# Two more groups of token pairs with seven products each, and the exits and squares shared between two engines

## The chip, the core and the metric

The kernel runs on one core of a Trainium2 chip. The metric is the device time of one execution in microseconds (us); lower is better. The engines are called as the profile calls them: PE is the matrix engine, DVE the vector engine, ACT the scalar engine, POOL the GpSimd engine, SP the engine that issues most DMAs. Each works through its own list of instructions in order and waits on semaphores of the others.

## What is computed

```python
scores = q @ k.transpose(0, 1, 3, 2) / 8              # q, k, v: (8, 12, 448, 64)
x = (np.maximum(scores, 0) ** 2 / 448 @ v)            # then heads side by side: (8, 448, 768)
u = x + np.real(fft(fft(x, axis=1), axis=2))
un = (u - mean(u)) / sqrt(var(u) + 1e-6)              # over the last axis
out = u + np.maximum(un @ w_ch1, 0) @ w_ch2           # 768 -> 3072 -> 768
```

An attention with squared relu, a Fourier mix over tokens and channels, and a feed-forward network (FFN) over 3584 tokens.

## The kernel before

**Order.** The order of work is written by a planner inside the kernel. Each piece of work is a generator that yields `need(engine, duration, dependencies, buffers)`; `Streams.run` (L80) picks the piece that can start first and issues its instructions. So the order on each engine is fixed when the program is built, from the planner's own durations; on the chip only semaphores move it.

**Attention** (`attention`, L526). Per batch 24 score blocks of 112 keys x 2 heads x 448 queries, in visits of up to three: six score matmuls (L591), then ACT takes the relu out of PSUM (L615) and DVE squares it in place (L621). Four squares feed one value product of 8 matmuls (L574) into a `psF` bank, of which there are two, shared with the FFN. DVE takes that product out in two halves of 224 columns (L475 and L479, in `fold`, L466) and folds it (L498, L500). SP turns the halves with DMA transposes (L521). There are 9 buffers for squares up to batch 3, and 6 from batch 4.

**Mix** (`mix` L1023, `mix_rows` L860). Channel transform (L1039), then for two chunks of rows the token transform (L868), a sum and a difference (L877, L879), the sum with x into `u` (L888, L890 on POOL and DVE), statistics (L903), and the normalized `un` (L920 on POOL; for batch 1 L923 on ACT, and turned by PE into `unT` at L837 and L842). `u` and `un` go to DRAM (L942 by SP, L945 by POOL); from batch 2 on `un` comes back turned by DMA (`turns`, L968, L986). `u` and `un` have two sets of buffers up to batch 3 and one from batch 4.

**FFN** (`ffn`, L1194). Tokens go in 12 groups: 384, 512, 384 and then nine of 256. Per group the first product (L1243, 24 rows of 128 hidden channels) goes through a relu (L1218 on ACT; in group 0 half of them L1216 on DVE) into `hT`. The second product of the first three groups is plain (L1274): 48 matmuls of 384 columns per block of 128 tokens. A group of 256 is one *pair* of blocks (class `Pair`, L1330): with the hidden channels halved (even and odd) and the output halved, the 2x2x2 block product is done with seven block products instead of eight, 84 matmuls instead of 96. That needs sums of hidden blocks, made by DVE for every pair (`early` L1312 to L1316, `late` L1324), and sums of weight blocks, made once by DVE (`weight_sums`, L1127), in buffers that other things have left. L1229 (DVE) adds each product to `u` in the output buffer `o`.

Of the kernel before, what the change touches and what calls it, by code (L numbers as in the profile page):

```python
# [62 lines left out]
class Streams:  # L63
# [9 lines left out]
    def dma(self, start, nbytes, rate=350e3, queue="hw"):  # L73
        slow = queue == "hw" and self.dma_free["sw"] > start + 2.0
        self.dma_free[queue] = max(self.dma_free[queue], start + 1.0) + nbytes / rate * (2.0 if slow else 1.0)
        if slow:
            self.dma_free["sw"] += nbytes / rate
        return self.dma_free[queue] + (3.0 if slow else 2.2 if queue == "sw" else 1.2)

# [63 lines left out]
def kernel(  # L143
# [27 lines left out]
    GT = [0, 384, 896] + list(range(1280, B * S + 1, 256))  # L171
# [129 lines left out]
    def home(i):  # L301

        return (i - NG) % 2 if i < 4 * NG else 1
# [96 lines left out]
    def turning():  # L400

        for b in range(B):
            for g in range(NG):
# [5 lines left out]
                for x in range(2):  # L409
                    e = yield need("DVE", 0.42, [ready[b * NG + g][x]], [BQR] if x == 0 else [])  # L410
                    o = work.tile([R, 4, HG, Dh], BF16, name="qkr", tag=f"qkr{x}", bufs=QR)
                    nc.vector.tensor_copy(o, loads[b * NG + g][x])  # L412
                    if b * NG + g != 4 * NG - 1:
                        BQ[x][home(b * NG + g)].free.append(e)
                    else:
                        qk_left.t = e + LATENCY["DVE"]
                    qk.append(o.rearrange("p c h d -> p (c h d)"))
# [48 lines left out]
    def fold(b, m, F, av, av_end):  # L466
# [4 lines left out]
        def leave():  # L471

            t = yield need("DVE", 2 * dve(HS) + 2 * dve2(NS) if one else dve(HS), [av_end],
                           [BX[m]] + ([BA[m]] if m < 3 else []))
            nc.vector.tensor_scalar(x[:, 0:HS].rearrange("q (p j) -> q p j", j=4), at[:, 0:R // 2],  # L475
                                    1.0 / (64.0 * S), None, op0=ALU.mult)
            t = yield from next_step(b, "DVE", dve(HS), t)
            xb, ab = x[:, XH + 1:XH + NS].rearrange("q (p j) -> q p j", j=4), at[:, R - 1:R // 2 - 1:-1, ::-1]
            nc.vector.tensor_scalar(xb, ab, 1.0 / (64.0 * S), None, op0=ALU.mult)  # L479
            t2 = t - 2 * dve2(NS) if one else t  # L480
            BF.give(av, t2)
            if b > 0:
                sch.add(turn_x(b, m, t2 + LATENCY["DVE"]), (1, 1))
            else:
                x_ready[b][m].t = t + LATENCY["DVE"]
            gone.t = t
            return t

        if one:
            e1 = yield from leave()  # L490
        else:
            sch.add(leave(), (0, 0))
            yield need("SP", 0.0, [gone])
            e1 = gone.t
        f = work.tile([128, 2, NS], BF16, name="fold", bufs=1,
                      tag=f"diff{m - 3}" if b == 0 and m >= 3 else f"fold{min(m, 3)}")
        e1 = yield from next_step(b, "DVE", dve2(NS), e1)
# [17 lines left out]

    def turn_x(b, m, t):

        e = yield need("SP", 0.5, [t], [BXN] if m == 0 else [])
        if m == 0:
            xns[b] = work.tile([128, 4, D], BF16, name="xn", tag="xn", bufs=1)  # L520
# [5 lines left out]
    def attention(b):  # L526


        F, sqs, fresh = [], {}, []
        if b == 4:  # L530
# [6 lines left out]
        while pa < NB:  # L537
            few = b == 0 or progress[0] == 0.0
# [7 lines left out]
            values = values or not n  # L546
            fresh.append(p + n)
            deps, bufs, dur = [], [], 0.0
            if values:
                deps += [sqs[i][1] for i in range(pa, pa + 4)]  # L550
# [3 lines left out]
                deps.append(ready[b * NG + ma // 2][2])  # L554
# [5 lines left out]
            lead = b + (p if n else pa) / NB - LEAD  # L560
# [5 lines left out]
            for part in ("scores", "values") if few else ("values", "scores"):  # L566
                if part == "values" and values:
                    av = BF.take()
                    vn, h0 = loads[b * NG + ma // 2][2], 2 * ma % HG
                    for c in range(4):  # L570
                        sq, _, at = sqs.pop(pa + c)
# [6 lines left out]
                    if ma % 2 == 1:  # L578
                        BQ[2].free.append(e)
                    pa += 4  # L580
# [22 lines left out]
            if scs:  # L603
                sch.add(squares(scs, sqs), (0.2, 0.2))
            if av_end is not None:
                yield from fold(b, ma, F, av, av_end)

    def squares(scs, sqs):
        for i, sc, t in scs:
# [7 lines left out]
            sch.add(square(r, e + LATENCY["ACT"], sqs[i][1]), (0.2, 0.2))  # L617

    def square(r, t, done):
        e = yield need("DVE", dve2(2 * S), [t])  # L620
        nc.vector.tensor_tensor(r, r, r, op=ALU.mult)  # L621
        done.t = e + LATENCY["DVE"]

    def attentions():
        for b in range(1, B):
            yield from attention(b)
# [4 lines left out]
    def side(b, ch):  # L631

        return ch if b < 4 else 1
# [226 lines left out]
    def mix_rows(b, ch, pcs):  # L860
# [3 lines left out]
        e = yield need("PE", 4 * mm(KN), [pcs[0][1], pcs[1][1]], [BS])  # L864
# [7 lines left out]
        e = yield need("ACT", act(KN), [e + LATENCY["PE"]], [BTS])  # L872
# [35 lines left out]
        e = yield need("DVE", 0.3, [e3 + LATENCY["ACT"]], [BUN[ch if b < 4 else 0]])  # L908
# [5 lines left out]
        for i, u in enumerate(us):  # L914
# [3 lines left out]
            un = work.tile([128, D], BF16, name="un", tag=f"un{2 * (ch if b < 4 else 0) + i}", bufs=1)  # L918
# [31 lines left out]
    def u_store(b, ch, us, ut, freed):  # L950
        yield from store_rows(ch, utop[b], ubot[b], us, 4, ut, u_stored[b])
        yield need("SP", 0.0, freed)
        for i in range(2):
            t = max(u_stored[b][2 * ch + i].t, freed[i].t)
            BU[i][side(b, ch)].free.append(t)
            if b == 3 and ch == 0:
                u_left[i].t = t

    def n_store(b, ch, t):
        yield from store_rows(ch, ntop[b], nbot[b], uns[b][2 * ch:2 * ch + 2], 2,  # L960
                              [t, t], n_stored[b])
        if b > 0:
            if b == 3 and ch == 1:
                un_left.t = n_stored[b][3].t
            else:
                BUN[ch if b < 3 else 0].free.append(n_stored[b][2 * ch + 1].t)

    def turns():  # L968

        pair_homes = None  # L970
        for k in range(2, NGR):
            t, g = GT[k], None
            while t < GT[k + 1]:
# [5 lines left out]
                e = yield need("SP", 1.5, deps, [BUNT] if g is None else [])  # L979
                if g is None and k == 2:  # L980
                    g = work.tile([128, MC, 512], BF16, name="unT", tag="unT0", bufs=1)
# [10 lines left out]
    def second_turned():  # L992
# [4 lines left out]
        BUN[1].free.append(e)  # L997
        group_ready[1].t = e
# [87 lines left out]
    PLAIN = (0, 1, 2)  # L1086
# [11 lines left out]
    unt_left, w2_free = Cell(), Cell()  # L1098
# [5 lines left out]
    def weight_sums():  # L1104
# [38 lines left out]
        yield from several(1, b12, b12, b11, ALU.subtract, [w2_free])  # L1143
        t4 = upper(JC * 256, KP, DH)
        yield from several(4, [(t4, i) for i in range(KP)], b21, t2, ALU.subtract, [w2_free])

    def uses():

        at, odd = [], 0
        for g in range(NGR):  # L1150
            n = (GT[g + 1] - GT[g]) // 128
            for c in range(0, n, 1 if g in PLAIN else 2):
                if g in PLAIN:
                    at += [(g, c, hf, (0, 1, 2, 3, 5)[(len(at) + hf) % 5]) for hf in range(2)]
                else:
                    at += [(g, c, 0, 0), (g, c + 1, 0, 1 + odd), (g, c + 1, 1, 3 + odd), (g, c, 1, 5)]
                    odd = 1 - odd
        return at
# [35 lines left out]
    def ffn(b):  # L1194
# [4 lines left out]
        flat = hid[0].rearrange("p j n -> p (j n)")  # L1199
        h = hid[0] if b in PLAIN else flat[:, 0:JC * 256].rearrange("p (j n) -> p j n", n=256)  # L1200
        ht = [Cell() for _ in range(JC)]
        work_us = JC * MC * mm(N) + NC * (2 * JC - (0 if b in PLAIN else KP // 2)) * mm(DH)
# [7 lines left out]
        def relu(ph, e, j):  # L1210

            en = "DVE" if b == 0 and j % 2 else "ACT"
            e = yield need(en, (dve if en == "DVE" else act)(JN * N), [e + LATENCY["PE"]], BH[j:j + JN])
            hs, ps = h[:, j:j + JN, 0:N], ph[:, 0:JN * N].rearrange("p (j n) -> p j n", j=JN)
            if en == "DVE":
                nc.vector.tensor_scalar(hs, ps, 0.0, None, op0=ALU.max)  # L1216
            else:
                nc.scalar.activation(hs, ps, AF.Relu)  # L1218
# [3 lines left out]

        left = {(c, hf): 1 if b in PLAIN or (c % 2, hf) == (0, 1) else 2 for c in range(NC) for hf in range(2)}

# [12 lines left out]
        for j in range(0, JC, JN):  # L1237
# [9 lines left out]
            if j == JC // 2:  # L1247
                ffn_begun[b].t = e
                if b not in PLAIN:
                    pairs = [Pair(b, c, h, ht, add, advance) for c in range(0, NC, 2)]  # L1250
                    for p in pairs:
                        sch.add(p.early(), (0, 0.3))
                        sch.add(p.late(), (0, 0.3))
        if b == 2:
# [4 lines left out]
        if b not in PLAIN:  # L1259
            for p in pairs:  # L1260
                sch.add(p.chain_a(), (4, 0))
                sch.add(p.chain_b(), (3.9, 0))
                yield need("SP", 0.0, p.done)
            for x in BH:
                x.free.append(max(d.t for d in p.done))
            return
        for c in range(NC):
            for hf in range(2):
                for jq in range(4):
# [3 lines left out]
                    for j in range(6 * jq, 6 * jq + 6):  # L1273
                        nc.tensor.matmul(pc[:, 0:DH], lhsT=h[:, j, c * 128:(c + 1) * 128], rhs=w2(j, hf),  # L1274
# [5 lines left out]
        if b == 2:  # L1280
            w2_free.t = e + LATENCY["PE"]

    class Pair:
# [14 lines left out]
        def early(self):  # L1298
# [110 lines left out]
    LEAD = 2.6  # L1409
# [50 lines left out]
```

## Time and profile before

| | us |
|---|---|
| runs shown: median, lowest to highest | 593.81, 592.65 to 594.01 |
| the profiled execution's own time | 595.38 |
| its span (first to last instruction) | 593.6 |
| PE busy in the span | 581.6 (98%) |
| DVE, ACT, POOL busy | 400.7, 292.4, 158.8 |
| matmuls of the second product: L1274, L1330 | 480, 756 |

Times below are from the span's start. "Busy" of PE is the time in which a matmul is under way. "Granted clock" is the share of full speed that PE was given.

### The profile page before, as it was taken

How to read it: one execution, taken by the hardware profiler on the slowest of the kernel's cores; microseconds unless marked ns; L12 is line 12 of the kernel's file. 1: busy time of each engine (PE TensorE's matmuls, PEld its weight loads, DVE VectorE, ACT ScalarE, POOL GpSimd, SP SyncE). 2: the span in 40 equal slices, each digit the busy share in tenths (PEclk: the TensorE clock that was granted, in tenths of full speed). 3: DMA queues.
4: the chain of work that ended last, by engine and by line, in shares of the span. 5: the costliest groups of instructions: out<-in, count | busy, mean ns of one | idle time of the engine just before them, and what ended most of it. 6: DMA issues, size and time to landing. Idle time of an engine off the chain costs nothing.

```text
span 593.6 us, 11558 instructions
## 1 busy us (share of the span) xinstructions
PE 581.6 (98%) x4522; PEld 370.8 (62%) x4522; DVE 400.7 (68%) x925; ACT 292.4 (49%) x433; POOL 158.8 (27%) x200
## 2 busy tenths in 40 slices
PE   8999999989999999999999999999999999999997
PEld 6566556534455465556757667566675686868684
DVE  6976775954678768877986877767898576232323
ACT  5966672467645557544617536275276340404040
POOL 8433112410236117312641134301260025000000
PEclk9998999989999999999999999999999999999999
DMA  9999999845958998888559967749264134221111
GB/s 126 207 210 228 210 213 143 190 81 90 170 117 177 208 141 216 136 162 136 141 141 166 140 127 207 126 100 175 102 181 87 53 120 151 75 84 47 66 43 53
DMA packets 133493, 82.29 MB, mean 139 GB/s; under 512 B 77504, under 2 KB 128608, under 8 KB 133440
## 3 DMA queue, kind: packets, MB, share of 16 engines
q0 software_dynamic: 40320, 34.07, 36.6%
q1 hardware_dynamic: 93120, 47.50, 35.2%
q8 instruction: 35, 0.57, 0.4%
q14 instruction: 18, 0.15, 0.1%
HBM read 62.91 MB, written 26.69 MB: 151 GB/s over the span
## 4 chain that ended last, share of the span: by engine, by line
PE 88%; DVE 5%; ACT 3%; POOL 2%; issue 2%; DMA 0%; DVEq 0%; POOLq 0%
PE psF L1243 35%; PE psF L1330 20%; PE psF L1274 13%; PE psF L574 7%; PE psS L591 6%; PE psS L1039 2%; ACT sq L615 2%; DVE sq L621 1%; PE psS L868 1%; PE psS L667 1%; POOL un L920 1%; PE psS L1014 1%; PE psF L448 0%; DVE o L1229 0%; DMA out_dram<-o 0%
## 5 line engine op out<-in xcount | busy, mean ns | idle before, releaser
L1243 PE MATMUL psF<-unT,w 128*128 128x256 bf16 (+2 forms) x1728 | 231.7, 292 | 1.8 <-ACT unT L842 1.7
L615 ACT ACTIVATE sq<-psS 112x896 bf16<-112x896 f32 x192 | 164.5, 916 | 93.3 <-PE psS L591 89.9
L1243 PEld LDWEIGHTS <-w 128*128 128x128 bf16 x1728 | 166.2, 98 | 64.5 <-issue 18.5
L1218 ACT ACTIVATE hT<-psF 128x512 bf16<-128x512 f32 (+1 forms) x168 | 96.7, 576 | 119.8 <-PE psF L1243 117.5
L621 DVE TENSOR_TENSOR sq<-sq 112x896 bf16<-112x896 bf16 x192 | 118.9, 633 | 36.1 <-ACT sq L615 35.6
L1330 PEld LDWEIGHTS <-hT 128*128 128x128 bf16 x648 | 62.9, 98 | 43.8 <-issue 2.3
L1274 PE MATMUL psF<-w,hT 128*128 128x384 bf16 x480 | 82.1, 326 | 0.0
L1229 DVE TENSOR_TENSOR o<-psF,o 128x384 f32<-128x384 f32 x83 | 45.8, 552 | 45.7 <-PE psF L1330 40.7
L1330 PE MATMUL psF<-w,hT 128*128 128x384 bf16 x378 | 66.4, 326 | 1.4 <-DVE xT L479 0.8
L1274 PEld LDWEIGHTS <-hT 128*128 128x128 bf16 x480 | 45.5, 98 | 34.5 <-issue 6.1
L591 PE MATMUL psS<-qkT 64*128 64x448 bf16 (+1 forms) x384 | 50.9, 359 | 1.6 <-ACT qkT L453 0.4
L319 POOL DMA_DIRECT2D vn<-in_v_dram x24 | 17.3, 720 | 115.6 <-PE psS L591 82.6
L574 PE MATMUL psF<-sq,vn 112*64 112x448 bf16 x384 | 45.5, 358 | 0.5 <-ACT hT L1218 0.5
L920 POOL TENSOR_SCALAR un<-u,rstd,nmr 128x768 bf16<-128x768 f32 (+1 forms) x24 | 29.6, 1241 | 42.4 <-DVE nmr L912 42.3
L475 DVE TENSOR_SCALAR xT<-psF 128x224 bf16<-128x224 f32 x48 | 18.6, 388 | 31.1 <-PE psF L574 30.6
L888 POOL TENSOR_TENSOR u<-tp,xn 128x385 f32<-128x385 f32 (+1 forms) x14 | 13.7, 978 | 84.0 <-DVE tp L877 76.5
L591 PEld LDWEIGHTS <-qkT 64*128 64x128 bf16 (+1 forms) x384 | 16.1, 102 | 28.2 <-issue 21.2
L574 PEld LDWEIGHTS <-vn 112*64 112x64 bf16 x384 | 17.8, 109 | 21.0 <-issue 12.1
L319 POOL DMA_DIRECT2D qn<-in_q_dram x21 | 15.1, 719 | 54.8 <-DVE qkr L412 46.1
L1330 PE MATMUL psF<-wsum,hT 128*128 128x384 bf16 x162 | 28.6, 326 | 0.0
L903 DVE BATCH_NORM_STATS2 stats<-u 128x6 f32<-128x384 f32 (+1 forms) x56 | 28.6, 539 | 0.0
L945 POOL DMA_INDIRECT ubot<-u,back x16 | 18.2, 1137 | 24.1 <-DVE sq L621 19.6
(141 smaller groups left out, 526.7 us busy)
## 6 DMA issues: line engine op xcount, KB each, us to landing
out_dram<-o SPq DMA_DIRECT2D x56, 192.0 KB
vn<-in_v_dram POOLq DMA_DIRECT2D x24, 224.0 KB, 5.4
qn<-in_q_dram POOLq DMA_DIRECT2D x21, 224.0 KB, 5.3
kn<-in_k_dram POOLq DMA_DIRECT2D x21, 224.0 KB, 8.1
w<-in_moe_w_ch_dram POOLq DMA_DIRECT2D x12, 384.0 KB, 13.2
w<-in_moe_w_ch_dram POOLq DMA_DIRECT2D x4, 1152.0 KB, 27.4
utop<-u SPq DMA_DIRECT2D x8, 384.0 KB
o<-utop SPq DMA_DIRECT2D x16, 192.0 KB
```

Of the source, the lines that this page charges most:

```text
L319: nc.gpsimd.dma_start(out=t, in_=src[b, hs].rearrange("h (p j) d -> p h (j d)", j=4))
L574: nc.tensor.matmul(av[h * Dh:(h + 1) * Dh, 0:S], lhsT=vn[:, c, h0 + h, :], rhs=sq[:, h, :], start=(c == 0), stop=(c == 3))
L591: nc.tensor.matmul(sc[:wide, h, 0:S].rearrange("k (c q) -> k c q", c=4), lhsT=flat[ps, k0:k0 + wide], rhs=qT[ps, m % 2], start=True, stop= ...
L615: nc.scalar.activation(r, sc[:R, :, 0:S], AF.Relu)
L621: nc.vector.tensor_tensor(r, r, r, op=ALU.mult)
L903: nc.vector.bn_stats(stats[:n, hf, :], u[:n, hf * (D // 2):(hf + 1) * (D // 2)])
L920: nc.gpsimd.tensor_scalar(un[:n], u[:n], rstd[:n, i:i + 1], nmr[:n, i:i + 1], op0=ALU.mult, op1=ALU.add)
L1218: nc.scalar.activation(hs, ps, AF.Relu)
L1229: nc.vector.tensor_tensor(o, pc[:, 0:DH], o, op=ALU.add)
L1243: nc.tensor.matmul(ph[:, i * N:(i + 1) * N], lhsT=w1_sb[m][hf][:, (jj + i) * 128:(jj + i + 1) * 128], rhs=unT[:, m, 0:N], start=(m == 0), ...
L1274: nc.tensor.matmul(pc[:, 0:DH], lhsT=h[:, j, c * 128:(c + 1) * 128], rhs=w2(j, hf), start=(j == 0), stop=(j == JC - 1))
L1330: nc.tensor.matmul(pc[:, 0:DH], lhsT=lhs[i], rhs=rhs[i], start=(start and i == 0), stop=(i == KP - 1), skip_group_check=True)
```

## The change

The last group now has 384 tokens and the third 256: groups are 384, 512, nine of 256, 384. Pairs begin with group 1: its first two blocks are a pair, its other two are done *whole*. In the last group two blocks are a pair and one is whole. Only group 0 stays plain. A whole block has 48 matmuls and an extra DVE add: as the weight sum of the upper and lower output half replaces one of the weight blocks in place, one product is shared by both halves. Everything that was switched at batch 4 (room for squares, single buffers of `u`, `un`, q and k) is switched at batch 2 (`ONE`) or batch 3 (`ONEQ`), since weight sums lie in those buffers earlier. From batch 1 on the second half of each exit of x is taken by ACT, and a square goes to ACT where the planner finds that sooner: 9 of 192. The last value product of a batch may wait for the first visit of the next.

```diff
-    GT = [0, 384, 896] + list(range(1280, B * S + 1, 256))
+    GT = [0, 384] + list(range(896, B * S - 383, 256)) + [B * S]
+    ONE, ONEQ = 2, 3
...
-        return (i - NG) % 2 if i < 4 * NG else 1
+        return (i - NG) % 2 if i < ONEQ * NG else 1
...
+            if b == 0:
...
+            else:
+                t = yield need("DVE", dve(HS), [av_end], [BX[m]] + ([BA[m]] if m < 3 else []))
+                nc.vector.tensor_scalar(xa[0], xa[1], 1.0 / (64.0 * S), None, op0=ALU.mult)
+                t2 = yield need("ACT", act(HS), [av_end])
+                nc.scalar.activation(xb[0], xb[1], AF.Copy, scale=1.0 / (64.0 * S))
+                t = max(t, t2 + LATENCY["ACT"] - LATENCY["DVE"])
...
-        room = NSQ if b < 4 else NSQ - 3
+        room = NSQ if b < ONE else NSQ - 3
...
+    def sooner(t, other, d, usual, du):
+
+        wait = {en: max(t, sch.engine[en]) + sch.queued(en) for en in (other, usual)}
+        return wait[other] + d + SPARE < wait[usual] + du
+
+    def square(b, r, t, done):
+        if b >= ELASTIC[0] and sooner(t, "ACT", act(2 * S), "DVE", dve2(2 * S)):
+            e = yield need("ACT", act(2 * S), [t])
+            nc.scalar.activation(r, r, AF.Square)
+        else:
+            e = yield need("DVE", dve2(2 * S), [t])
+            nc.vector.tensor_tensor(r, r, r, op=ALU.mult)
...
-        return ch if b < 4 else 1
+        return ch if b < ONE else 1
...
-        e = yield need("PE", 4 * mm(KN), [pcs[0][1], pcs[1][1]], [BS])
+        e = yield need("PE", 4 * mm(KN), [pcs[0][1], pcs[1][1]], [BS, BTS])
...
-    PLAIN = (0, 1, 2)
+    WHOLES = [[0, 1, 2], [2, 3]] + [[]] * (NGR - 3) + [[2]]
+    PAIRS = [[], [0]] + [[0]] * (NGR - 2)
...
+        yield need("DVE", 0.0, [upper_free])
         t4 = upper(JC * 256, KP, DH)
...
+            if b == 1:
+                moves = [(halves[:, :, j], ph.rearrange("p (x n) -> p x n", x=2))]
+            elif b == NGR - 1:
+                moves = [(h[:, j], ph[:, 0:256]), (block(j, 2), ph[:, 256:384])]
...
+    def whole(b, c, ht, block, add, advance):
+
+        def products(pc, k, weights, start, i0, i1):
+
+            for i in range(i0, i1):
+                nc.tensor.matmul(pc[:, 0:DH], lhsT=block(2 * i + k, c), rhs=weights[i],
+                                 start=(start and i == 0), stop=(i == KP - 1), skip_group_check=True)
+            advance((i1 - i0) * mm(DH))
+
+        half = KP // 2
+        d = half * mm(DH)
+        w11, w21, w22 = ([w2(2 * i + k, hf) for i in range(KP)] for k, hf in ((0, 0), (1, 0), (1, 1)))
+        yield need("PE", d, ht[0:KP:2], [BF])
+        pc = BF.take()
+        products(pc, 0, w11, True, 0, half)
+        e = yield need("PE", d, ht[KP::2])
+        products(pc, 0, w11, True, half, KP)
+        both = Cell()
...
+        sch.add(first(), (0, 0))
+        yield need("PE", d, [sums[1]] + ht, [BF])
+        pd = BF.take()
+        products(pd, 0, T[1], True, 0, half)
+        for k, w, i0 in ((0, T[1], half), (1, w22, 0), (1, w22, half)):
+            e = yield need("PE", d)
+            products(pd, k, w, False, i0, i0 + half)
+        sch.add(add(pd, e, c, 1), (0, 0))
+        yield need("PE", d, [both])
+        products(pc, 1, w21, False, 0, half)
+        e = yield need("PE", d)
+        products(pc, 1, w21, False, half, KP)
+        sch.add(add(pc, e, c, 0), (0, 0))
...
-                yield need("DVE", d, self.ht[2 * i0:2 * i1] + self.waits)
+                yield need("DVE", d, self.ht[2 * i0:2 * i1] + self.waits + ([upper_free] if k else []))
```

More of the change, by code (lines that the diff above doesn't have):

```diff
@@ L78, in dma, with queued @@
         return self.dma_free[queue] + (3.0 if slow else 2.2 if queue == "sw" else 1.2)
+    def queued(self, eng):
+        n = 0.0
+        for s in self.streams:
+            if not s[2] or s[2][0] != eng:
+                continue
+            _, dur, deps, bufs, ok = s[2]
+            ts = [d.t if isinstance(d, Cell) else d for d in deps]
+            if all(t is not None and t <= self.engine[eng] for t in ts) and all(len(p.free) >= bufs.count(p) for p in bufs):
+                n += dur
+        return n
     def run(self):
@@ L549, in attention @@
             if values:
[L550 removed]
+                deps += [sv[i][1] for i in range(4 * mv, 4 * mv + 4)]
                 bufs.append(BF)
@@ L1248, in ffn @@
                 ffn_begun[b].t = e
[L1249 to L1254, printed above, removed]
+                pairs = [Pair(b, c, h, ht, add, advance) for c in PAIRS[b]]
+                for p in pairs:
+                    sch.add(p.early(), (0, 0.3))
+                    sch.add(p.late(), (0, 0.3))
+        if b == 0:
             unt_left.t = e
@@ L1257, in ffn @@
             BUNT.free.extend([e, e] if b == 1 else [e])
[L1259 to L1267, printed above, removed]
+        for c in WHOLES[b]:
+            if b > 0:
+                yield from whole(b, c, ht, block, add, advance)
+                continue
             for hf in range(2):
```

167 lines of the change are left out of this document (100 added, 67 removed).

## The prediction

> **What bounds the kernel now.** First the busy times and the slices of the page.
>
> ```profile
> span 593.6 us, 11558 instructions
> ...
> PE 581.6 (98%) x4522; PEld 370.8 (62%) x4522; DVE 400.7 (68%) x925; ACT 292.4 (49%) x433; POOL 158.8 (27%) x200
> ...
> PE   8999999989999999999999999999999999999997
> ```
>
> PE is busy nearly always. "Busy" is no proof of work, so I read next where PE waits, in the list of waits for PE alone.
>
> ```profile
> PE psF L1243 <- ACT unT L842: 1.7, 1, 1.7
> PE psS L1405 <- DVE warm L230: 1.3, 1, 1.3
> PE psS L770 <- ACT un L746: 0.9, 1, 0.9
> PE psF L1330 <- DVE xT L479: 0.8, 1, 0.8
> PE psF L1330 <- DVE o L1229: 0.6, 1, 0.6
> ```
>
> Two of the five lie before 52 us, where the change does nothing. The others are the start of group 1 (1.7), the first pair (0.8, at 299 us) and a later pair (0.6, at 426 us). The last stage of the chain that ended last is PE alone:
>
> ```profile
> 560.71 15.72 PE psF L1243 x144
> 576.42 13.66 PE psF L1330 x84
> ```
>
> 84 matmuls in 13.66 us: **0.163 us** per matmul of 384 columns. So the end is set by PE's work plus its few waits. A matmul less is time less, unless a wait takes its place. The table by stretch (columns after the stretch and its length: PE, PEld, DVE, ACT, POOL busy, then granted clock) shows where a wait is near:
>
> ```profile
> 90.00:105.00 15.00, 15.00 (x108) 9.63 (x106) 9.02 (x19) 2.10 (x4) 3.81 (x5) 1.00 0.87 139
> 105.00:120.00 15.00, 15.00 (x105) 8.59 (x104) 12.86 (x31) 8.33 (x12) 5.59 (x6) 1.00 0.91 189
> 120.00:135.00 15.00, 12.81 (x76) 5.52 (x75) 9.02 (x22) 10.03 (x14) 2.12 (x3) 0.89 0.58 90
> ```
>
> **PE's work.** In the order of instructions of the changed build, the first product (L1243) has the same matmuls: 1296 of 256 columns, 288 of 384, 144 of 512. Attention and mix are the same too. The second product goes from 480 + 756 to 288 + 924 matmuls: eleven pairs instead of nine at 12 saved each, and whole blocks with 48 like plain ones. That is 24 x 0.163 = **-3.9 us**.
>
> **DVE.** Added: two pairs' sums of hidden blocks (per pair the three shapes of L1312, L1314, L1316 and L1324, 1.26 + 1.48 + 1.25 + 1.25 = 5.2), so 10.5; nine adds of 0.552 (L1229), 5.0. Removed: 42 second halves (L479, 0.384), 16.1; nine squares (L621, 0.633), 5.7. Net -6.3 us in all; DVE does not bound on average, but its places move (below).
>
> **ACT.** 42 exits: no row shows ACT with 224 columns. L1218 takes 0.492 for 384 and 0.598 for 512, so by that slope 0.36, and 0.384 (DVE's) is the other bound: some 15 us. Nine squares: below, L621's 0.633; above, L615's 0.916 (same shape from PSUM); I take 0.9 as the same engine, 8 us. The last group's relu is two instructions, 24 x (0.39 + 0.28 - 0.49), 4 us, under six matmuls of 1.0 us. ACT was busy 292 of 594 us, so PE and DVE hide all three, except where ACT stands in a chain.
>
> The halves do not run side by side: in the built program the ACT half waits for DVE's half just ahead of it, and the first fold for ACT's. So an exit takes 0.39 + 0.36 and two hand-overs, against 0.30 + 0.38 before (start to end in the rows at 299 us). The Trainium skill (PSUM — Partial Sum Buffer, PSUM bank collisions raise a hardware error) says why: two engines on the same bank and quadrant, reads included, must be kept apart by a semaphore. If they ran together an exit would take 0.4 us; no run here shows that. Either way a bank is back before PE needs it, some 2 us later (a score visit of 0.68 and 12 matmuls of 256 columns in the other bank, 1.3). Between the halves DVE can stand for 0.4 us: cost nothing where DVE has idle time, counted in the seam below.
>
> **Single buffers from batch 2.** Before had them from batch 4, and PE's waits above show none in batches 4 to 7. I cost them at nothing; the cover is the distance between a mix and the group that reads it. Without it, a late group: see groups 2 and 3 below.
>
> **The seam to group 1 (before: 123.8 to 125.6 us).** Before, PE has 0.23 + 0.23 + 1.73 us of waits here, as ACT takes three relus (2.53 us from 122.44) ahead of the last cast of `unT` (L842, 0.67). Then the clock drops:
>
> ```profile
> 124.00:124.50 0.50, 0.00 (x0) 0.00 (x0) 0.47 (x4) 0.50 (x2) 0.00 (x0) 1.00 0.22 46
> 125.50:126.00 0.50, 0.44 (x2) 0.16 (x2) 0.50 (x2) 0.01 (x1) 0.00 (x0) 0.50 0.58 117
> 129.00:129.50 0.50, 0.50 (x4) 0.19 (x2) 0.00 (x0) 0.00 (x0) 0.00 (x0) 1.00 0.86 184
> ```
>
> Twelve matmuls of 512 take 4.26 us instead of 2.65 (the next 24 take 5.29): 1.6 us more. In the changed order the same relus stand ahead of the same cast, and one exit's ACT half ahead of them. Counted from batch 1's first channel matmul, PE has 25.0 us of work up to group 1 (108 matmuls at 0.163, mix 3.3, three score visits 2.0, a value product 0.9, turns 1.2), and the last score visit starts at 22.8. In before, from that visit to group 1 is 125.56 - 122.03 = 3.53. Added: the ACT half 0.36, the DVE half ahead of it 0.39, and some 0.8 as seven pieces of weight sums (L1127, 0.35 to 0.75) stand around it on DVE. 22.8 + 3.53 + 1.55 = 27.9, so 2.9 us idle against 2.2: **+0.7**, and the half clock stays.
>
> **The pair in group 1.** Its weight sum in the upper half of `hT` and two thirds of its hidden sums must wait until the whole blocks are read. DVE has about 9 us of work from there, PE 10 to 14: about 0.4 late. What goes is the 0.8 at 299 us, where the weight sums were made beside the first pair. Net **-0.4**.
>
> **Group 3.** It now needs 64 tokens of batch 3. In the changed order PE has 19.4 us from batch 3's first L868 to group 3. In before, from L868 to the store of `ntop` it was 10.1, 15.3 and 9.8 us (batches 3 to 5), to the turning DMA another 3.3 (360.20 to 363.47), its issue 1.2, and its landing is in no row: 0 below, 5.4 above (the landing of `nbot`). I take 2, as these are 64 rows. On SP the turn is now queued behind an output store that waits for the last add of group 2's pair: 16.3 + 0.2 + 0.55 + 0.35 = 17.4. Then 17.4 + 1.2 + 2 = 20.6: **+1.2** (bounds: 0 and 5.8). Group 2 has 2 to 6 us to spare: from batch 2's first L868 to it PE has 38.8 us of work, and in before's batches 2 to 7 the last store of `nbot` was issued 22 to 27 us after L868; 5.4 for its landing, two turns of 1.25 and again 2 make 32 to 37. Groups 4 to 11 have over 10 by their place in the order.
>
> **Sum**: -3.9 + 0.7 - 0.4 + 1.2 = -2.4 us. Against the profiled execution's own 595.38 us (span 593.6 and 1.8 around it) that is 593.0; the median of the runs shown, 593.81, lies 1.6 below that execution, so the forecast is **591.4 us**, from 590 to 592.5 in its own case. It is just beyond 0.3% (1.8 us), about what a measurement of this kernel can tell from no change.
>
> **Rivals.**
> *Slower: DVE becomes the bound at the seam.* Thirteen pieces of weight sums (3.3 and 3.4 us by the L1127 rows) move from 244 to 255 us into 90 to 120 us, where DVE was busy 21.9 of 30. 28.6 of 30 leaves little, and batch 1's sums, statistics and casts stand behind them. If all 6.7 us come ahead of the last cast, -3.9 + 6.7 gives 596.6. It decides once more than 3.9 us of them are exposed. Against it: 8.1 us of DVE idle time there, and the planner ranks them last. 0.16.
> *The gain is eaten.* Group 3 late by 3 to 5 us instead of 1.2: 593.2 to 595.2; with 3.5 it is 593.7. For: the upper bounds above. 0.24.
> *The clock stays full at the seam.* The row at 125.5 us speaks against it, unless the wait shrinks: -2.4 - 1.6 gives 589.8. The Trainium skill (TensorE: Matmul & The Clock Gate, What's actually happening) puts the drop after an idle window of about 3.4 us; by that a wait of 2.9 us keeps the clock, but here it fell at waits of 2.2. 0.10.
>
> **Chances.** Forecast 0.50, the others as said. Of the forecast's case 0.04 lies above 592.0 and counts as same: faster 0.56, same 0.28, slower 0.16. The range 589.0 to 595.6 takes in the eaten gain, most of the full-clock case and the lower part of the slower one.
>
> **What would show it.** Right: 924 + 288 matmuls in the second product; PE busy about 578; a wait at group 1 of 2 to 3 us with half clock behind it; one at group 3 of about 1. Wrong: a wait of over 4 us at group 1 with DVE full before it; waits on turned `unT` at groups 2 or 3 of over 3 us; many short waits of PE on `psF` banks held by the exit's ACT half.

## The result, and the profile after

The changed kernel took 599.74 us (median of 6 runs, 598.79 to 603.58) against 593.91 for the kernel before on the same chip: a ratio of 1.0112 over all runs (not of the two medians), 95% interval 1.0082 to 1.0142. Forecast were 591.4 us, 589.0 to 595.6. The profiled execution took 601.27 us, its span is 599.5.

The same lines of the page as for before: span, busy times, and the rows of PE and of the granted clock in 40 slices of 15 us.

```profile
span 599.5 us, 11496 instructions
...
PE 580.5 (97%) x4493; PEld 370.5 (62%) x4498; DVE 398.2 (66%) x907; ACT 310.7 (52%) x508; POOL 153.8 (26%) x200
...
PE   8999999989999999899998999999999999999997
...
PEclk9998999999999999889998999999999999999999
```

PE's row now has digits below 9 in the middle, and the clock's row has 8s there. Slices 17 (240 to 255 us) and 22 (315 to 330) have both; slice 9 (120 to 135), the seam, has an 8 for PE and a full clock. PE's work at the end is as counted: 48 matmuls of a whole block in 7.80 us, 84 of a pair in 13.66. So the loss is not there.

```profile
551.13 23.40 PE psF L1305 x144
574.53 7.80 PE psF L1354 x48
582.33 13.66 PE psF L1434 x84
```

The list of PE's waits (total, times, longest) names what came in between. Lines of the changed kernel: L1305 is the first product, L1434 a pair, L601 the value product, L496 the exit's half on ACT, L659 the square on DVE, L881 the cast of `unT` on DVE, L1291 the add to `o`, L1279 the relu of the first product.

```profile
PE psF L1434 <- ACT xT L496: 2.3, 3, 1.9
PE psF L601 <- DVE sq L659: 1.9, 2, 1.1
PE psF L1434 <- DVE o L1291: 1.4, 1, 1.4
PE psF L1305 <- DVE unT L881: 0.9, 1, 0.9
PE psF L1305 <- DMA unT<-ntop: 0.9, 1, 0.9
PE psF L1305 <- ACT xT L496: 0.7, 1, 0.7
```

From 54 us on, waits of PE over 0.2 us sum to 10.6 us, before to 4.1. By place:

| | before | changed |
|---|---|---|
| seam to group 1 (123 to 127 us) | 2.2, and 1.6 for half clock | 1.6, full clock |
| group 2 (215 to 218) | none | 0.72 + 0.62 |
| group 3 (249 to 253) | none | 1.10 + 0.82 + 0.85, and 2.7 for half clock |
| pair of group 4 (319.5; before: the first pair, 299.8) | 0.78 | 1.93, and 1.8 for half clock |
| a later pair | 0.65, at 426.4 | 1.36, at 511.9 |

The 2.7 is the length of the 48 matmuls behind group 3's stop, 7.93 us (below), less 48 at the pace of the 144 in 15.72 us of the prediction's chain. The 1.8 is the length of the 12 matmuls behind the pair's stop, 3.79 us (below), less 12 at 0.163. Sum against the profile of before: -3.9 of work, +6.5 of waits, and for the clock +2.2 (0.989 against 0.994, at 1.3 us for each 0.003; the price is derived with the table of all runs below). That is 4.8 of the 5.9 us by which the spans differ. By the lengths in the table the clock costs 2.7 + 1.8 - 1.6 = 2.9 instead of 2.2. So 0.4 to 1 us stays unassigned.

**The seam** went better than forecast. By stretch (PE, PEld, DVE, ACT, POOL busy, granted clock): DVE is nearly full ahead of it, as the slower rival had it, and yet the clock stays at 1.00. The third row shows the half clock at group 3.

```profile
105.00:120.00 15.00, 15.00 (x104) 8.77 (x103) 14.63 (x32) 10.07 (x14) 6.14 (x6) 1.00 0.62 170
120.00:135.00 15.00, 13.40 (x87) 6.03 (x87) 12.64 (x29) 11.47 (x18) 2.97 (x5) 1.00 0.80 121
...
253.00:255.00 2.00, 2.00 (x10) 1.37 (x10) 1.52 (x3) 1.15 (x2) 1.70 (x3) 0.50 0.67 140
```

**Group 3** is late. In PE's order of time (start, length, wait in brackets), a visit of attention stands just ahead of it; its value products wait for squares that DVE has just been given, and then the rows turned by DMA are still missing. The rows of SP show when the turning transfer was issued:

```profile
249.52 0.38 PE L601 MATMUL psF<-sq,vn 112*64 112x448 bf16 x2 [1.10 <-DVE sq L659]
250.72 0.38 PE L601 MATMUL psF<-sq,vn 112*64 112x448 bf16 x2 [0.82 <-DVE sq L659]
...
252.94 7.93 PE L1305 MATMUL psF<-unT,w 128*128 128x256 bf16 x48 [0.85 <-DMA unT<-ntop]
...
247.54 0.33 SPq L1225 DMA_DIRECT2D out_dram<-o  x1
247.97 1.21 SPq L1022 DMA_TRANSPOSE unT<-ntop  x1
```

The rows came last, at 252.94, 4.97 us after their transfer was issued. Without the waits for squares PE would have stood for the rows instead, for the same 2.8 us in all.

**Group 2** waits for neither rows nor squares. On DVE a copy (L425) that waited 2.50 us for a DMA transpose stood ahead of an exit's first half. So ACT waited 2.64 us for that half, and PE 0.72 for ACT's. The other 0.62 is for a relu that stood on ACT behind two relus of scores.

**The pair of group 4** waits 1.93 us for the exit's ACT half. But ACT waited for DVE's half, and DVE was late. The rows of DVE, ACT, PE and POOL, each by time:

```profile
314.68 0.84 DVE L1416 TENSOR_TENSOR hT<-hT 128x256 bf16<-128x256 bf16 x1 [0.15 <-ACT hT L1279]
315.56 0.96 DVE L1418 TENSOR_TENSOR hT<-hT 128x256 bf16<-128x256 bf16 x1
...
317.69 1.06 DVE L425 COPY qkr<-kn 112x1024 bf16<-112x1024 bf16 x1
318.67 0.38 DVE L494 TENSOR_SCALAR xT<-psF 128x224 bf16<-128x224 f32 x1
...
319.08 0.36 ACT L496 ACTIVATE xT<-psF 128x224 bf16<-128x224 f32 x1 [1.53 <-DVE xT L494]
...
319.50 3.79 PE L1434 MATMUL psF<-w,hT 128*128 128x384 bf16 x12 [1.93 <-ACT xT L496]
...
313.81 2.57 POOL L959 TENSOR_SCALAR un<-u,rstd,nmr 128x768 bf16<-128x768 f32 x2 [7.60 <-DVE nmr L951]
316.46 1.03 POOL L927 TENSOR_TENSOR u<-tp,xn 112x385 f32<-112x385 f32 x1
```

Alone, these sums take 0.28 to 0.29 us and the copy 0.42. While POOL makes `un` and `u` they take 0.84 to 1.06. At 504.6 to 507.8 us it is the same: three sums of 512 (0.42 alone) take 1.00, 1.09 and 1.13 us, and the pair waits 1.36 at 511.9. The totals of busy time hide it: a slowed DVE counts as busy.

### The profile page after: what moved, and what is told of

Read it like the earlier page. It is cut to its first block, busy times and chain, and to the rows that moved or that the text cites. A ratio compares the mean times of both kernels' runs of the same rounds, so it can differ in the third digit from the quotient of the medians.

```text
span 599.5 us, 11496 instructions
## 1 busy us (share of the span) xinstructions
PE 580.5 (97%) x4493; PEld 370.5 (62%) x4498; DVE 398.2 (66%) x907; ACT 310.7 (52%) x508; POOL 153.8 (26%) x200
## 4 chain that ended last, share of the span: by engine, by line
PE 79%; DVE 9%; ACT 4%; DMA 3%; issue 3%; POOL 1%; SPq 0%; DVEq 0%; POOLq 0%; ACTq 0%
PE psF L1305 35%; PE psF L1434 20%; PE psF L601 6%; PE psS L619 5%; PE psF L1330 4%; PE psF L1354 3%; PE psS L1074 2%; ACT sq L644 2%; DVE sq L659 2%; PE psS L907 1%; DMA qkT<-qkr 1%; DVE o L1291 1%; DMA out_dram<-o 1%; DMA unT<-ntop 1%; PE psS L706 1%
## 5 line engine op out<-in xcount | busy, mean ns | idle before, releaser
L1305 PE MATMUL psF<-unT,w 128*128 128x256 bf16 (+2 forms) x1723 | 233.6, 293 | 3.6 <-DVE unT L881 0.9
L1305 PEld LDWEIGHTS <-w 128*128 128x128 bf16 x1728 | 166.9, 99 | 68.2 <-issue 18.6
L644 ACT ACTIVATE sq<-psS 112x896 bf16<-112x896 f32 x192 | 167.1, 920 | 28.2 <-PE psS L619 28.1
L1279 ACT ACTIVATE hT<-psF 128x512 bf16<-128x512 f32 (+2 forms) x192 | 99.1, 529 | 89.0 <-PE psF L1305 88.8
L659 DVE TENSOR_TENSOR sq<-sq 112x896 bf16<-112x896 bf16 x183 | 113.8, 634 | 36.4 <-ACT sq L644 36.1
L1434 PEld LDWEIGHTS <-hT 128*128 128x128 bf16 x792 | 77.5, 98 | 55.5 <-issue 7.0
L1434 PE MATMUL psF<-w,hT 128*128 128x384 bf16 x462 | 83.2, 331 | 2.1 <-ACT xT L496 2.1
L1291 DVE TENSOR_TENSOR o<-psF,o 128x384 f32<-128x384 f32 x92 | 50.7, 552 | 50.5 <-PE psF L1434 41.9
L496 ACT ACTIVATE xT<-psF 128x224 bf16<-128x224 f32 x42 | 15.2, 361 | 85.5 <-DVE xT L494 84.9
L601 PE MATMUL psF<-sq,vn 112*64 112x448 bf16 x384 | 45.9, 359 | 3.1 <-DVE sq L659 1.9
L959 POOL TENSOR_SCALAR un<-u,rstd,nmr 128x768 bf16<-128x768 f32 (+1 forms) x24 | 27.2, 1139 | 51.7 <-DVE nmr L951 51.6
L1434 PE MATMUL psF<-wsum,hT 128*128 128x384 bf16 x198 | 34.6, 326 | 0.2 <-ACT xT L496 0.2
L494 DVE TENSOR_SCALAR xT<-psF 128x224 bf16<-128x224 f32 x42 | 16.2, 386 | 26.9 <-PE psF L601 26.7
L332 POOL DMA_DIRECT2D qn<-in_q_dram x21 | 15.3, 730 | 70.3 <-DVE qkr L425 62.2
L601 PEld LDWEIGHTS <-vn 112*64 112x64 bf16 x384 | 18.0, 109 | 24.3 <-issue 16.3
L1330 PE MATMUL psF<-w,hT 128*128 128x384 bf16 x144 | 25.1, 326 | 0.1
L1354 PE MATMUL psF<-w,hT 128*128 128x384 bf16 x144 | 24.2, 326 | 0.0
```

The source lines that it names most:

```text
L332: nc.gpsimd.dma_start(out=t, in_=src[b, hs].rearrange("h (p j) d -> p h (j d)", j=4))
L601: nc.tensor.matmul(av[h * Dh:(h + 1) * Dh, 0:S], lhsT=vn[:, c, h0 + h, :], rhs=sq[:, h, :], start=(c == 0), stop=(c == 3))
L644: nc.scalar.activation(r, sc[:R, :, 0:S], AF.Relu)
L1291: nc.vector.tensor_tensor(o, pc[:, 0:DH], o, op=ALU.add)
L1305: nc.tensor.matmul(ph[:, i * N:(i + 1) * N], lhsT=w1_sb[m][hf][:, (jj + i) * 128:(jj + i + 1) * 128], rhs=unT[:, m, 0:N], start=(m == 0), ...
L1330: nc.tensor.matmul(pc[:, 0:DH], lhsT=block(j, c), rhs=w2(j, hf), start=(j == 0), stop=(j == JC - 1))
```

## The experiments

Three theories stood at the start. **A**: POOL slows DVE, so sums and exits come late at pairs. **B**: group 3 needs batch 3's first 64 tokens too early. **C**: the exit in two halves on two engines holds the `psF` banks. A fourth, **D**, came up on the way. "Planned anew" means that the planner wrote another order for the edited kernel, so that other things moved too; e5 and e6 keep the order.

**e1.** `un` on ACT:

```diff
-            en = "POOL" if b > 1 else "ACT"
+            en = "ACT"
...
```

> The changed kernel with the normalized rows un made by ACT instead of POOL in batches 2 to 7 (the order is planned anew). In the changed kernel DVE's sums of hidden blocks took two to three times as long while POOL made un or u (0.84 to 1.13 us instead of 0.28 to 0.43, at 314 to 318 and at 504 to 507 us), and PE then waited 1.93 us at 319.5 and 1.36 at 511.9, the first with half clock behind it (1.6). Theory A (DVE is slowed by POOL, and that is what makes PE wait): both waits and the half clock go, -4 to -5 us against the changed kernel's 599.7: 595 to 596. Theory B (the third group is late, nothing else matters): the 2.8 us before group 3 stay and so does the time, 599 to 601. Theory C (the exit in two halves, DVE then ACT, holds the psF banks): ACT has 22 us more, the halves come later, 601 to 604.

600.26 us, ratio 1.0113 (1.0089 to 1.0138). The waits at the pairs were gone (0.29 at 318.4 us, then nothing over 0.21), as A has it. But group 3 cost 6.0 us of waits in place of 2.8: in the new order its rows came still later, 6.4 us after their transfer was issued instead of 5.0. A is right on its places. On the sum it was wrong: the forecast of 595 to 596 missed, as group 3 took the gain.

**e2.** Both exit halves on DVE:

```diff
-                t2 = yield need("ACT", act(HS), [av_end])
-                nc.scalar.activation(xb[0], xb[1], AF.Copy, scale=1.0 / (64.0 * S))
-                t = max(t, t2 + LATENCY["ACT"] - LATENCY["DVE"])
+                t = yield from next_step(b, "DVE", dve(HS), t)
+                nc.vector.tensor_scalar(xb[0], xb[1], 1.0 / (64.0 * S), None, op0=ALU.mult)
```

> The changed kernel with both halves of every exit on DVE again, as before the change (planned anew). DVE gets 16 us more work, ACT 15 us less. Theory A: DVE's sums come later still, 602 to 606. Theory B: no change, 599 to 601. Theory C: PE's waits on the ACT half (0.72 at 215.5 and 1.93 at 319.5 us, with 1.6 of half clock) go, 595 to 597.

606.0 us, ratio 1.0212 (1.0178 to 1.0246). PE waited 8.05 us for the rows of group 3, after 1.29 and 1.97 for squares. The two waits that C names, at 215.5 and 319.5, went, but 11.3 us came at group 3, so the time went the other way than C had it. As a cause of the loss C falls. In this order the ACT half is worth 6 us; that it gets batch 3 through DVE earlier is the likely reason, not a shown one.

**e3.** No square on ACT:

```diff
-    LEAD, SPARE, ELASTIC = 2.6, 0.5, (1, 0)
+    LEAD, SPARE, ELASTIC = 2.6, 0.5, (99, 0)
```

> The changed kernel with every square on DVE (planned anew). Nine squares of 0.63 us go back to DVE, nine of about 0.9 leave ACT. Theory A: DVE later by 5.7 us in sum, some of it at a pair or a visit: 600 to 603. Theory B: 599 to 601. Theory C: ACT's halves come a little earlier: 598 to 600.

605.45 us, ratio 1.0181 (1.0151 to 1.0212), above all that was expected: 2.43 + 1.79 + 0.42 us of waits for squares at 257 to 261 us, and 2.92 at 203.7, where DVE's add waited for a DMA into `o` (theory D below).

**e4.** Other rows for group 3:

```diff
+                if k == 3 and bb == 3:
+                    bb = 2
```

> The changed kernel, but the last 64 tokens of group 3 are read from batch 2's normalized rows (long stored) instead of batch 3's, so the output is wrong for these 64 tokens and group 3 does not wait for batch 3's mix; planned anew. Theory B: the 2.8 us of waits before group 3 and the half clock behind them (1.6) go: -4.4, 595.3. Theory A and C: the waits only move by what is filled in there, 598.5 to 600.

592.99 us, ratio 0.9985 (0.9967 to 1.0004): 6.7 less than the changed kernel. No stop before group 3. But the waits of 1.93 and 1.36 at the pairs had gone too, and one of 1.93 stood at 215.5 us: the order had moved. So the run does not separate B from the pairs' waits, and does not give its size.

**e5.** The same data in the changed kernel's order:

```diff
+                if k == 3 and bb == 3:
+                    src = ntop[2]
```

> As e4 the last 64 tokens of group 3 are read from batch 2's normalized rows, but the order of all instructions is that of the changed kernel: the planner still counts on batch 3. What is left of the loss is the order alone. In the changed kernel PE has 1.10 + 0.82 us of waits for squares and 0.85 for the turned rows before group 3, and half clock after (1.6). Theory B1 (the transfer's lateness is the cost): 0.85 goes and the clock holds, -2.5, 597. Theory B2 (the cost is the order, in which attention is drawn forward to fill the stop that the planner foresees, so that it waits for squares): at most -0.9, 599. Theory A: 599 either way.

600.15 us, ratio 1.0110 (1.0088 to 1.0131). 1.11 + 0.82 + 0.45 us of waits stayed. That fits B2 by its number, but the rows of SP show that the transfer was not earlier:

```profile
248.54 0.33 SPq L1227 DMA_DIRECT2D out_dram<-o  x1
...
248.91 1.23 SPq L1024 DMA_TRANSPOSE unT<-ntop  x1
```

It stands in the same place of SP's list, behind an output store that follows the last add of group 2's pair, and was issued 5.1 us before group 3 starts (253.99), as in the changed kernel (5.0). So the run shows that batch 3's own store is not what the transfer waits for: SP's order is. B1 and B2 are not told apart by it.

**e6.** `un` on ACT, in the changed kernel's order (the planner still counts on POOL):

```diff
-            if b > 1:
-                nc.gpsimd.tensor_scalar(un[:n], u[:n], rstd[:n, i:i + 1], nmr[:n, i:i + 1],
-                                        op0=ALU.mult, op1=ALU.add)
-            else:
-                nc.scalar.activation(un[:n], u[:n], AF.Identity, bias=nmr[:n, i:i + 1],
-                                     scale=rstd[:n, i:i + 1])
+            nc.scalar.activation(un[:n], u[:n], AF.Identity, bias=nmr[:n, i:i + 1],
+                                 scale=rstd[:n, i:i + 1])
```

> As e1 (un on ACT), but in the order of the changed kernel. Theory A: the waits at 319.5 us (1.93 and 1.6 of half clock) and at 511.9 (1.36) go; at group 3 un is now queued behind ACT's relus, 0 to 1.5 us later than on POOL. Together -3.5 to -5: 595 to 596.5. If POOL's un is not what delays DVE there: 599.5 or more, with the waits in place.

598.03 us, ratio 1.0071 (1.0045 to 1.0098). The sums that took 0.84 and 0.96 us, and the copy, are back at their own lengths, and the pair waits 0.29 instead of 1.93:

```profile
313.48 0.29 DVE L1412 TENSOR_TENSOR hT<-hT 128x256 bf16<-128x256 bf16 x1 [0.16 <-ACT hT L1275]
313.81 0.29 DVE L1414 TENSOR_TENSOR hT<-hT 128x256 bf16<-128x256 bf16 x1
...
314.55 0.42 DVE L425 COPY qkr<-kn 112x1024 bf16<-112x1024 bf16 x1
...
316.65 1.62 PE L1430 MATMUL psF<-w,hT 128*128 128x384 bf16 x9 [0.29 <-ACT xT L496]
```

That shows A's mechanism with the order of PE, DVE and SP unchanged. The gain, 1.7 us, is smaller than the 3.5 to 5 expected, as a new wait of 1.61 us for a relu on the fuller ACT stands at 451.7. Group 3 stays as it was (1.03 + 0.82 + 1.03).

**e7.** Attention earlier:

```diff
-    APART = 1.3
+    APART = 0.7
```

> The changed kernel with one number changed: visits of attention may follow each other after 0.7 us of FFN work on PE instead of 1.3, so batch 3's attention and mix come earlier (planned anew). Theory B: no wait and no half clock before group 3, -4.4 us; some 1 to 2 us of new waits about 125 and 205 us, where attention now is denser: 596 to 597. Theory A: the late sums stay where POOL meets them, 599 or more.

597.62 us, ratio 1.0076 (1.0054 to 1.0098). No wait at group 3: the turning transfer is issued 8.8 us before the group starts, instead of 5.0. A new wait, 3.04 + 0.65 us, stands at 205 to 209.

**e8.** e7 and e1 together:

```diff
-    APART = 1.3
+    APART = 0.7
...
-            en = "POOL" if b > 1 else "ACT"
+            en = "ACT"
...
```

> e7 and e1 together: attention after 0.7 us, un on ACT, planned anew. If A and B are both causes, and add: 599.7 - 4.4 - 4 + 1.5 of new waits = 592.5 to 593.5. If only B: as e7. If only A: as e1, 599 to 601.

594.18 us, ratio 0.9999 (0.9980 to 1.0017), 0.7 above the answer for two causes that add. Both are causes, but they do not simply add: together they gain 5.6 us, alone e7 gained 2.1 and e1 lost 0.5. What was left was mostly one place, the pair of group 1. DVE waits 4.26 us for a DMA, and PE for DVE; the rows of SP show the store of the buffer's last content and its next load:

```profile
206.80 3.57 PE L1430 MATMUL psF<-w,hT 128*128 128x384 bf16 x12 [3.32 <-DVE o L1287]
...
206.19 0.56 DVE L1287 TENSOR_TENSOR o<-psF,o 128x384 f32<-128x384 f32 x1 [4.26 <-DMA o<-utop]
...
196.49 0.53 SPq L1221 DMA_DIRECT2D out_dram<-o  x1
...
200.62 0.38 SPq L1217 DMA_DIRECT2D o<-utop  x1
```

The load was issued late and took over 5 us to land, with three DMA transposes issued on SP between 197 and 202 (whether these slowed it was not tried). That is theory **D**: the change's whole blocks and its pair in group 1 use the same output buffers right after each other.

**e9.** Other buffers first, all else in e8's order but SP:

```diff
-        at, odd, n = [], 0, 0
+        at, odd, n = [], 1, 0
```

> e8 with one digit changed: the pairs of groups 1, 3, 5 and so on use output buffers 2 and 4 instead of 1 and 3, and those of groups 2, 4, 6 the reverse. PE, DVE, ACT and POOL keep exactly their order; only SP's differs. In e8 the largest wait left is 3.32 + 0.65 us at 206.8 us (and half clock behind it): DVE's add in group 1's pair waits 4.26 us for the DMA that brings rows of u into an output buffer whose last content, from the whole block just ahead, was stored at 196.5 us and which was filled again only from 200.6. Theory D (the buffer's reuse is the cost): both waits and the half clock go, 594.2 - 4 - 1.5 = 588.5 to 590.5, faster than the kernel before. If another transfer or DVE is late there anyway: 593 to 594.5.

**589.25 us**, ratio 0.9930 (0.9909 to 0.9952): faster than both kernels. From the page:

```profile
span 587.2 us, 11469 instructions
...
PE 574.9 (98%) x4498; PEld 368.9 (63%) x4498; DVE 388.4 (66%) x905; ACT 334.0 (57%) x534; POOL 125.1 (21%) x176
```

No wait after 54 us is longer than 0.9, and the clock is full. As PE, DVE, ACT and POOL keep e8's order, D holds.

**e13**, made to see whether e9 is carried by `un` on ACT alone: e7 and the digit of e9, `un` on POOL:

```diff
-    APART = 1.3
+    APART = 0.7
...
-        at, odd, n = [], 0, 0
+        at, odd, n = [], 1, 0
```

> e7 and the one digit of e9 together, un on POOL as in the changed kernel: group 3's stop and the late output buffer are away, DVE's slowing by POOL stays. It tells whether the three causes add. If they do: 597.6 - 3.04 - 0.65 - 1.4 (half clock) = 592.5, and the waits of 0.76 and 1.36 us at 316.8 and 505.4 us stay; the remaining distance to e9's 589.25, 3.3, is then un on POOL. If un on ACT was what made e9 fast and the buffer mattered only with it: 596 to 598.

594.27 us, ratio 1.0010 (0.9989 to 1.0031), between the two answers. The wait at 205 us shrank to 2.05, now behind a copy on DVE that waits for a DMA transpose. Of the waits at pairs that of 1.36 stayed, and e7's 0.76 grew to 1.57. So from 599.74, in this order of steps: earlier attention -2.1, fresh buffer -3.4, `un` off POOL -5.0. With the last two exchanged (e7, e8, e9) it is -2.1, `un` -3.4, buffer -4.9, so the sizes depend on the order of steps. Without the buffer (e8) or without `un` (e13) it is 594; leaving out the earlier attention alone was not tried.

**e10.** The kernel before with the second half of the exits on ACT from batch 1, the fold waiting for both halves as in the change:

```diff
-            nc.vector.tensor_scalar(xb, ab, 1.0 / (64.0 * S), None, op0=ALU.mult)
+            if b == 0:
+                nc.vector.tensor_scalar(xb, ab, 1.0 / (64.0 * S), None, op0=ALU.mult)
...
+            else:
+                t2 = yield need("ACT", act(HS), [av_end])
+                nc.scalar.activation(xb, ab, AF.Copy, scale=1.0 / (64.0 * S))
...
```

> The kernel before with one part of the change alone: from batch 1 on the second half of each exit is taken by ACT (planned anew). The prediction costed this at nothing: 593.4 to 594.6. Theory C (the serial halves hold the banks): short waits on ACT's half before pairs, 595 to 597. If the relief of DVE by 16 us is worth something in itself, as e2's 6 us the other way say: 591 to 593.

602.86 us, ratio 1.0144 (1.0118 to 1.0170), a miss. One place costs 6 us: on DVE a copy that waits for a DMA transpose stands ahead of its half, so ACT waits 7.89, and PE 5.98 with half clock behind it (DVE, ACT and PE by time):

```profile
164.08 0.43 DVE L412 COPY qkr<-kn 112x1024 bf16<-112x1024 bf16 x1 [7.60 <-DMA qkT<-qkr]
...
164.89 0.36 ACT L483 ACTIVATE xT<-psF 128x224 bf16<-128x224 f32 x1 [7.89 <-DVE xT L475]
...
165.30 2.29 PE L1250 MATMUL psF<-unT,w 128*128 128x512 bf16 x5 [5.98 <-ACT xT L483]
```

The serial halves carry one engine's late DMA to a second engine, as they do at group 2 of the changed kernel (2.50, 2.64, 0.72). Whether a better order would make them free in the kernel before was not tried.

**e11.** The kernel before with single buffers from batch 2 or 3 (`un`'s homes, q and k likewise):

```diff
-        return (i - NG) % 2 if i < 4 * NG else 1
+        return (i - NG) % 2 if i < 3 * NG else 1
...
-        room = NSQ if b < 4 else NSQ - 3
+        room = NSQ if b < 2 else NSQ - 3
...
-        return ch if b < 4 else 1
+        return ch if b < 2 else 1
...
```

> The kernel before with another part alone: single buffers of u, un, q and k and six buffers for squares from batch 2 or 3 instead of batch 4 (planned anew). The prediction costed this at nothing: 593.4 to 594.6. If single buffers are what makes batches 2 and 3 late: waits before groups 2 and 3 of 1 to 4 us, 595 to 599.

592.65 us, ratio 0.9980 (0.9965 to 0.9995). Costed at nothing, and costs nothing with the old groups; two short waits even went.

**e12.** The kernel before with `un` on ACT:

```diff
-            en = "POOL" if b > 1 else "ACT"
+            en = "ACT"
...
```

> The kernel before with un on ACT in all batches (planned anew). Before, PE has 0.8 + 0.65 us of waits at pairs. If DVE's being slowed by POOL costs time only where pairs' sums are late, as theory A has it for the changed kernel: at most -1.4, 592.6 to 594.3. If the gains of e6 and e8 come from un on ACT as such: 590 to 592.

590.65 us, ratio 0.9957 (0.9941 to 0.9974). POOL slows DVE there too: DVE's busy time fell from 400.7 to 396.2 us with the same instructions in another order, and the two waits at pairs are gone. The time lies under the answer for A (592.6 to 594.3), in the range of the other one. At equal, full clock the span is 588.8 against 591.0: the two waits at pairs (1.4) explain the larger part of these 2.2 us, and 0.8 stays open. The rest of the 3.2 is the clock, which was full in 8 of 12 executions here and in 6 of 23 of the kernel before.

**All runs.** Waits are PE's over 0.2 us after 54 us; "rest" is the span without them and without 1.3 us for each 0.003 of mean granted clock below 1. That price comes from the runs of the kernel before: a span of 591.0 us at 1.000, 592.3 at 0.997, 593.6 at 0.994.

| | median | profiled span | clock | waits | rest |
|---|---|---|---|---|---|
| before | 593.91 | 593.6 | 0.994 | 4.1 | 586.9 |
| e10, exits | 602.86 | 602.5 | 0.991 | 12.1 | 586.5 |
| e11, buffers | 592.65 | 591.9 | 0.997 | 3.2 | 587.4 |
| e12, un | 590.65 | 588.8 | 1.000 | 2.7 | 586.1 |
| changed | 599.74 | 599.5 | 0.989 | 10.6 | 584.1 |
| e1 | 600.26 | 595.3 | 0.993 | 10.7 | 581.6 |
| e2 | 606.0 | 602.2 | 0.985 | 15.3 | 580.4 |
| e3 | 605.45 | 603.8 | 0.986 | 13.0 | 584.7 |
| e4 | 592.99 | 589.6 | 0.999 | 7.2 | 582.0 |
| e5 | 600.15 | 598.4 | 0.991 | 11.2 | 583.3 |
| e6 | 598.03 | 596.3 | 0.994 | 10.2 | 583.5 |
| e7 | 597.62 | 593.1 | 0.997 | 9.2 | 582.6 |
| e8 | 594.18 | 593.3 | 0.993 | 7.4 | 582.9 |
| e13 | 594.27 | 592.4 | 0.997 | 8.6 | 582.5 |
| e9 | 589.25 | 587.2 | 1.000 | 4.1 | 583.1 |

The fair match for e9 is e12, as both have `un` on ACT: 589.25 against 590.65 us. So of the 4.6 us by which e9 beats the kernel before, 1.4 are left when the kernel before gets the same mend for `un`.

## Why the prediction was wrong

**PE's work, -3.9: right.** The trace has the 924 and 288 matmuls. The rest is 586.1 to 587.4 us with the old groups and 580.4 to 584.7 with the new; the means differ by 3.9. At full clock and with `un` on ACT in both, e9's span is 587.2 against e12's 588.8, with 1.4 us more of waits: 3.0 less. What went wrong is what came on top. Against the forecast, group 3 cost 4.3 us more, the late pairs and the pair in group 1 together 4.1, group 2 1.3, and the seam 2.9 less: 6.8 of the 8.3 us between 591.4 and 599.74.

**The seam, +0.7 and half clock: wrong, on the pessimistic side.** 1.6 us of waits instead of 2.9, and full clock. The added ACT and DVE pieces (1.55 us) were all put into the chain to group 1; in the order that ran, they did not lengthen it. The full clock, which a rival had at 0.10, is in part luck: in e12 the waits of before, 0.23 + 0.23 + 1.73, left the clock at 1.00, and in the profile of before they halved it.

**The pair in group 1, -0.4: wrong on both parts.** No wait of 0.4 came in that pair (190 to 206 us). One of 0.36 at 187.5 lies near it, but there a value product waits for a whole block's add. And the 0.78 taken as gone at 299.8 us came back as 1.93 at 319.5.

**Group 3, +1.2: the first step that failed, a term that was mis-sized.** It cost 2.8 us of waits and 2.7 of half clock, 5.5 in all, at the upper end of the stated bounds of 0 to 5.8. The path was right: the transfer stood on SP behind the output store, and was issued 18.05 us after batch 3's first token transform (L907 at 229.92), 17.4 in the working. But from issue to PE's start it took 4.97 us, not 1.2 + 2, so the landing was 3.8 instead of 2. PE had 20.3 us of work, not 19.4, and 23.0 - 20.3 is the 2.8. The other part is half clock behind the stop, which was priced at the seam only. e7, where the transfer is issued 8.8 us ahead, has no wait there. The rival "the gain is eaten" had this place, at 3 to 5 us.

**"DVE does not bound", cost nothing: the second step that failed.** It went by a sum, -6.3 us of DVE work. DVE's busy time fell by 2.5 only; with `un` off POOL in both, from e12 to e6, it fell by 5.8. And what counts is where the late pieces lie: the late pairs cost 1.93 + 1.8 + 1.36 us, and e6 leaves 0.29 of the first wait and nothing of the last. The slowing is not new, as e12 shows; the change moved what stands behind it. The profile of before had the sign: a sum of 512 (L1314) took 1.02 us at 296.1, right beside POOL's `u`, against 0.42 alone, two squares around it 1.26 and 1.32 against 0.62, and the first pair waited just after them. I read that wait as one for weight sums. The Trainium skill (SBUF — State Buffer, Who interferes with whom) has the rule: a DVE instruction with two inputs in SBUF and a GpSimd instruction that reads SBUF shut each other out, the second waits until the first ends. The rows at 504 us agree: three sums in a row take 1.00 to 1.13 us, and each ends 0.27 or 0.28 us after the POOL instruction that was under way when it began (these took 0.96 to 1.14). And the add to `o`, with one input in PSUM, took 0.557 us (median) in the 9 cases that lay beside `un` or `u` on POOL and in the 83 that did not, as the same rule has it.

**ACT's exits and squares, single buffers, cost nothing.** Buffers: right with the old groups (e11). Exits and squares were not neutral: without them, planned anew, the kernel is 6 us slower each time, mostly at group 3 (e2, e3), with the old groups the exits cost 9 (e10), and at group 2 the serial halves passed on 0.72.

**Output buffers** were in no step. In the changed order D cost PE nothing (DVE's add waited 1.41 us for a load at 201.4, and PE did not); it came out when the rest was mended.

Of the signs of being wrong that were named, none came as written: DVE was nearly full ahead of the seam without a long wait there, the wait on turned rows showed as 0.85 us, as the rest lay in waits for squares, and only two waits on the ACT half were over 0.3 us.

Open stays the 0.4 to 1 us between the sum of waits and the span, and how much of e10's 9 us is the exits' own.

## What to carry to other kernels

Costing an added piece by the engine's busy total finds nothing where the order is fixed: look for the three or four places where the last input of the bounding engine is made, and ask what shares the maker's path just then, another engine's port included. A saving in work that arrives in full can still be lost: take waits and clock off the span of several variants, and see whether the rest has moved by what was counted. A stop is a step in a queue, too: here a transfer that needed nothing more still stood behind a store (e5), and what helped was the order of the work (earlier attention, another buffer). And when a mend helps the changed kernel, give it to the kernel before as well (e12), or the change is credited with it.

## What the runs showed of the hardware

Mean clocks of one kernel lie close to steps: 1.000, 0.997, 0.994, some 1.3 us of span apart. A drop follows a stop, though not always: the same three stops at the seam (0.23 + 0.23 + 1.73 us) halved the clock in the profiled execution of before and left it at 1.00 in that of e12. In e4 stops of 1.93 and 0.63 us left it at 1.00.

Not every DVE sum beside POOL is slowed; in some places POOL is slowed instead. In the changed kernel's profile six hidden sums of 256 and 512 beside `un` or `u` on POOL took two to three times their length, while two others of 256 and most fold sums (L518 and L520, with both inputs in SBUF) took 0.26 to 0.30 us, as alone. POOL's rows of `un` took 0.97 or 0.98 us in 12 of 24 cases. The one beside the fold sums at 314.1 us took 1.58, the one at 378.2 us 1.51, and that at 451.5 us 1.21. So in these places it was POOL that lost the time. No run set the order of the two engines to show which one waits.
